# Transposing r, a~ and W of four chunks within partitions, with the transposition finished by DMA over DRAM, in a chunked RWKV-7 plus gated MLP kernel on one Trainium2 core

## The chip, the core and the metric

The kernel runs on one core of one Trainium2 chip. A core has five engines, each with a queue of its own that issues in order: TensorE (PE in the profile; its weight loads are PEld), VectorE (DVE), ScalarE (ACT), GpSimd (POOL) and SyncE (SP). SP computes nothing; nearly all DMAs of this kernel are issued from its queue. The metric is the device time of one execution in microseconds. Three runs of the kernel before took 804.71, 801.88 and 800.59 us, median 801.88.

## The reference, cut to what matters

There are 4 batches and 8 heads, 768 steps and a head dimension of 40. Each head keeps a 40x40 state that every step reads, decays, corrects and extends:

```python
for t in range(S):
    y[:, :, t] = einsum('bhd,bhde->bhe', r[t], state)
    Sa = einsum('bhde,bhe->bhd', state, a[t])
    state = state * w[t][:, :, None, :] - outer(Sa, b[t]) + outer(v[t], k[t])
```

The result, reshaped to 3072 tokens of 320 features, goes through a two-layer block with the activation h cos h:

```python
h = x @ w_in            # 3072x320 by 320x2048
out = (h * cos(h)) @ w_out
```

All is float32.

## The kernel before

**Chunks.** The recurrence is cut into 24 chunks of 32 steps. Within a chunk the steps are worked off as matmuls: W is the running product of w from the chunk's start, a~ is a times W of the step before, b and k are divided by W. So each chunk needs r, a~, W, b/W, k/W and v with the head dimension on the partitions ("transposed": rows 0 to 39 and 64 to 103 hold the even and the odd heads), while DRAM gives them with batch and step on the partitions ("natural", tiles `nat_w`, `nat_a`, `nat_r` and so on, 40 features padded to 64).

**How the transposed form is made.** `turned` (line 327) issues four TensorE transposes of 128x128, two heads each, into a PSUM tile, and ScalarE or VectorE moves the result to SBUF. For W and a~ this goes two chunks at a time in phase 1:
- `p1_w(c)` (362): eight transposes of `nat_w` into `wT`; for chunks from 4 on ScalarE copies each half into a tile `wb` (378); POOL copies the last column of each head into `wc` (380) and writes ones into the first columns (`from_one`, 391). `over_w` (393) takes the reciprocal of the natural W on VectorE and multiplies b by it on POOL.
- `p1_a(c)` (406): eight transposes of `nat_a` into `aps`; VectorE multiplies each half by W into `aT` (`a_W`, 399).
- `p1_b(c)`, `p1_n(c)`: transposes of b/W, then the products of b/W with a~ into `nps`, which ScalarE copies into `nt` (459).

For r and v it is done chunk by chunk in `p2_v(c)` (604): four transposes each, from `vp` and `rp`, which POOL filled from `nat_v` and `nat_r` in `p2_in` (584), and two copies of ScalarE.

**Where W comes from.** For chunks from 4 on the running products are made four chunks at a time. `ws_fetch` (159) loads w of one "quad" into `ws`, a tile with (batch, head, chunk) on the 128 partitions and 32x40 values each; `ws_scan` (166) does nine VectorE multiplications along the steps; `ws_store` (178) writes the products to DRAM (`wd`), from where `load` brings them into `nat_w` chunk by chunk. `scanned(q)` (906) issues the scan, and by `later` the store two steps and the next fetch twelve steps on. It stands in chunk 3 for quad 2, at the end of chunk 4 for quad 3, and near the end of chunks 8 and 12 for quads 4 and 5.

**The order of work.** Nothing is scheduled by a compiler: instructions stand on each queue in the order of the program. For every chunk a list `segs` (lines 1049 to 1101) names the steps: `t` (transposes of the state), `q` (the state read by r), `x`, `s`, `z` (the solve and the new state), `v`, `k`, `g` (the next chunk's inputs and their Gram matrices), the phase-1 steps `pw`, `pa`, `pb`, `pn` of two chunks that lie some chunks ahead, and places `M` for pieces of the two-layer block. The chunks that carry `pw` and `pa` for chunks from 8 on are 4, 5, 7, 9, 11, 13, 15 and 17. `later(n, work)` (343) lets work be issued n steps on; DMAs are placed in this way.

The chain within a chunk that the prediction speaks of: `t` writes the transposed state to PSUM, ScalarE copies it (`s`, 658), `q` multiplies it with r, ScalarE copies that (`qz`, 670), `x` reads it (`x0ps<-qz,aT`), ScalarE and VectorE copy (`x`, 695 and 696), and `s` reads those (`sps`). Each M piece is 8 to 24 matmuls `ph` or `po`; ScalarE and VectorE turn `ph` into `gT` (829 to 839, "turns"). The big PSUM tiles (`wT`, `aps`, `qps`, `nps`, `kT`, `x0ps` and others) share two buffers in turn.

## Time and profile before

| what | value |
| --- | --- |
| runs shown | 800.59, 801.88, 804.71 us |
| profiled execution, from its first to its last instruction | 803.7 us |
| granted TensorE clock, mean | 0.973 |
| TensorE busy | 753.0 us (94%) |
| VectorE, ScalarE, POOL busy | 487.9, 387.2, 200.2 us |
| DMA packets of SP's queue | 177440, 30.1% of 16 engines |
| reciprocal of W on VectorE, 128x320 | 20 of 2.14 us |
| transposes wT, aps, r: median duration | 273 ns |

The profile gives the span of the profiled execution and no separate time of it. Times in a row of the timeline are the start and then the duration; "x8" means that eight equal instructions are shown as one row. Matmuls overlap, so the distance between starts of neighbouring rows says what a group takes from TensorE's queue, and not its duration. A bracket at the end of a row holds the idle time before it on its engine and what ended it. In the windows, each engine's busy time is followed by its number of instructions, and the last three numbers are the granted clock, the DMA share and GB/s. Rows named SPq are SP's DMA issues.

### The profile page before, as it was taken

To read this page: it belongs to the slowest core of one execution; us is meant where nothing else is said; L and a number is where in the kernel's file an instruction comes from. 1 tells how busy PE (TensorE), PEld (TensorE's weight loads), DVE (VectorE), ACT (ScalarE), POOL (GpSimd) and SP (SyncE) were. 2 spreads that over 40 slices of the span, in tenths; PEclk is the share of its full clock that TensorE was granted. 3 is DMA by queue.
4 is the path that set the end of the run, shared out by engine and by line. 5 is a ranking of instruction groups with operands and counts; after the bars stand their busy time and mean duration, and the time that the engine had idled before them with its cause. 6 is when DMAs were issued, how large, how long until landed. Compare 5 with 4: busy or idle time off the path is not lost.

```text
span 803.7 us, 39602 instructions
## 1 busy us (share of the span) xinstructions
PE 753.0 (94%) x17812; PEld 578.6 (72%) x17812; DVE 487.9 (61%) x1025; ACT 387.2 (48%) x723; POOL 200.2 (25%) x354
## 2 busy tenths in 40 slices
PE   4777799999989999999999999999999999999997
PEld 4545577777767777777777787777787777777775
DVE  8879858854634796553895644994346863333231
ACT  1337766554434436545435635534645445354352
POOL 5326634320321220330330230332031122201000
PEclk9778999999999999999999999999999999999999
DMA  8675462443253324334224314223220222001000
GB/s 113 164 187 141 132 171 64 91 93 66 50 122 55 71 40 68 68 99 69 54 44 68 91 40 69 52 44 71 45 46 21 46 46 53 20 16 34 20 17 16
DMA packets 183304, 55.79 MB, mean 69 GB/s; under 512 B 157152, under 2 KB 178656, under 8 KB 183136
## 3 DMA queue, kind: packets, MB, share of 16 engines
q1 hardware_dynamic: 177440, 52.11, 30.1%
q8 instruction: 140, 2.29, 1.2%
q10 hardware_dynamic: 5440, 0.82, 0.7%
q0 software_dynamic: 256, 0.33, 0.3%
q14 instruction: 28, 0.23, 0.1%
HBM read 42.07 MB, written 11.14 MB: 66 GB/s over the span
## 4 chain that ended last, share of the span: by engine, by line
PE 68%; DVE 14%; ACT 5%; DMA 5%; issue 4%; POOL 2%; SPq 2%; DVEq 0%; ACTq 0%; POOLq 0%
PE ph L101 24%; PE po L101 20%; PE x0ps L101 4%; PE dps L101 3%; DVE rw L395 3%; PE gram L101 3%; PE vT L330 3%; PE sps L101 2%; DVE inv_tmp L494 2%; DVE inv L498 2%; PE nps L101 2%; PE qps L101 2%; PE sT L654 1%; SPq L152 1%; PE kT L330 1%
## 5 line engine op out<-in xcount | busy, mean ns | idle before, releaser
L101 PE MATMUL po<-w_out_sb,gT 128*128 128x320 f32 x768 | 223.3, 439 | 0.0
L101 PE MATMUL ph<-xT,w_in_sb 128*128 128x256 f32 x768 | 187.8, 389 | 1.9 <-issue 1.9
L101 PEld LDWEIGHTS po<-w_out_sb,gT 128*128 128x128 f32 x768 | 140.1, 190 | 54.4 <-issue 2.0
L101 PEld LDWEIGHTS ph<-xT,w_in_sb 128*128 128x128 f32 x768 | 140.8, 192 | 31.9 <-issue 14.1
L829 ACT ACTIVATE turns<-ph,rnd 128x512 f32<-128x512 f32 x96 | 64.2, 685 | 159.9 <-PE ph L101 159.5
L831 DVE SCALAR_TENSOR_TENSOR turns<-turns,ph 128x512 f32<-128x512 f32 x96 | 64.1, 683 | 115.3 <-ACT turns L829 115.0
L839 DVE TENSOR_TENSOR gT<-ph,turns 128x512 f32<-128x512 f32 x96 | 65.7, 686 | 39.1 <-ACT turns L836 39.1
L755 POOL TENSOR_TENSOR qz<-qz,wc 128x160 f32<-128x160 f32 x92 | 42.1, 475 | 167.5 <-DVE qz L754 166.8
L836 ACT ACTIVATE turns<-turns,half_pi 128x512 f32<-128x512 f32 x96 | 69.3, 722 | 3.1
L835 ACT ACTIVATE turns<-turns 128x512 f32<-128x512 f32 x96 | 60.2, 627 | 18.9 <-DVE turns L831 18.9
L101 PE MATMUL ph<-xT,w_in_tail 64*128 64x256 f32 (+1 forms) x512 | 55.0, 393 | 2.7 <-issue 2.7
L498 DVE TENSOR_TENSOR inv<-inv,inv_tmp 128x31 f32<-128x31 f32 (+15 forms) x124 | 50.7, 409 | 4.3
L754 DVE TENSOR_TENSOR qz<-dps,qz 128x160 f32<-128x160 f32 x92 | 28.9, 314 | 35.5 <-PE dps L101 35.4
L586 POOL COPY vp<-nat_v 128x320 f32<-128x320 f32 x24 | 12.0, 500 | 153.7 <-DMA nat_v<-in_v_dram 133.1
L494 DVE TENSOR_TENSOR inv_tmp<-u,inv 128x31 f32<-128x31 f32 (+15 forms) x124 | 48.3, 390 | 2.3
L395 DVE RECIPROCAL rw<-nat_w 128x320 f32<-128x320 f32 x20 | 42.8, 2141 | 0.1
L658 ACT COPY s<-sT 128x512 f32<-128x512 f32 x46 | 24.5, 583 | 35.9 <-PE sT L654 35.9
L101 PEld LDWEIGHTS ph<-xT,w_in_tail 64*128 64x128 f32 (+1 forms) x512 | 32.2, 160 | 12.2 <-issue 8.6
L766 POOL TENSOR_TENSOR yt<-yt,wb 128x512 f32<-128x512 f32 x24 | 31.6, 1316 | 22.3 <-DVE yt L761 22.3
L396 POOL TENSOR_TENSOR bn<-nat_b,rw 128x320 f32<-128x320 f32 x22 | 19.9, 906 | 43.9 <-DVE rw L395 37.1
L642 ACT COPY vvm<-gram 128x256 f32<-128x256 f32 x24 | 8.8, 368 | 45.6 <-DVE ag L637 45.2
L718 DVE TENSOR_TENSOR sm<-sps,su 128x128 f32<-128x128 f32 x48 | 11.7, 284 | 31.1 <-ACT sm L713 28.4
(136 smaller groups left out, 1130.6 us busy)
## 6 DMA issues: line engine op xcount, KB each, us to landing
words<-in_moe_w_in_dram SPq DMA_DIRECT2D x8, 512.0 KB
xd<-yt SPq DMA_DIRECT2D x48, 80.0 KB
out_dram<-ot SPq DMA_DIRECT2D x24, 160.0 KB
nat_k<-in_k_dram SPq DMA_DIRECT2D x92, 40.0 KB
nat_v<-in_v_dram SPq DMA_DIRECT2D x92, 40.0 KB
nat_r<-in_r_dram SPq DMA_DIRECT2D x92, 40.0 KB
nat_a<-in_a_dram SPq DMA_DIRECT2D x84, 40.0 KB
ws<-in_w_dram SPq DMA_DIRECT2D x5, 640.0 KB
```

The costliest lines, as they stand in the source:

```text
L101: nc.tensor.matmul(o, lhsT=lhsT, rhs=rhs, start=start, stop=stop, skip_group_check=True)
L330: nc.tensor.transpose(ps[:, i * P : (i + 1) * P], x[:, 2 * i : 2 * i + 2].rearrange("p e d -> p (e d)"), ident)
L395: nc.vector.reciprocal(rw, wn)
L494: nc.vector.tensor_tensor(tmp, u[:, j : j + 1, :j].to_broadcast([P, C - j, j]), x[:, j:, j : j + 1].to_broadcast([P, C - j, j]), ALU.mult,)
L498: nc.vector.tensor_tensor(x[:, j:, :j], x[:, j:, :j], tmp, ALU.subtract)
L755: nc.gpsimd.tensor_tensor(z, z, wc.rearrange("p (f m b) -> p f m b", f=2, m=2)[:, :, :, bb] .unsqueeze(3).to_broadcast([P, 2, 2, D]), ALU. ...
L766: nc.gpsimd.tensor_tensor(yt.rearrange("p j b t -> p (j b) t"), yt.rearrange("p j b t -> p (j b) t"), wx, ALU.mult)
L829: nc.scalar.activation(n, u, ACTF.Identity, bias=rnd, scale=1.0)
L831: nc.vector.scalar_tensor_tensor(n, n, -ROUND, u, ALU.add, ALU.subtract)
L835: nc.scalar.activation(n, n, ACTF.Abs)
L836: nc.scalar.activation(n, n, ACTF.Sin, bias=half_pi, scale=-2.0 * math.pi)
L839: nc.vector.tensor_tensor(gT[:, 2 * e : 2 * e + 2].rearrange("p f t -> p (f t)"), us[e], ns[e], ALU.mult)
```

## The change

From chunk 8 on (`QT = 8`) r, a~ and W aren't transposed by TensorE any more.

- `quad_fetch` loads r or a of four chunks in the layout of `ws` into a tile `raw`. A flip then permutes each partition's 32x40 values to 40x32: `quad_r` and `quad_w` with one ScalarE copy, `quad_a` with one VectorE multiplication, which also makes a~ from a and W, and a small ScalarE copy for the first step. `quad_store` writes the flipped tile to DRAM one step later.
- `fetch_T` reads a chunk of it back, in two DMAs of 40 partitions by 16 runs of 32 values, straight into `wb`, `aT` or `rT`.
- `p1_w` and `p1_a` keep `over_w` for these chunks and issue the fetches instead of the transposes; `own_w` does POOL's share in the b step. `p2_v` transposes v alone. The natural loads of a and r go; those of w, b, k and v stay.
- In `scanned`, `quad_a` follows the scan at once, `quad_w` comes four steps on, and the next fetch goes from 12 to 14 steps. `quad_r` is issued six steps into chunks 5, 9, 13 and 17, its fetch one step into them.
- The free axis of `aT` and `wb` gets another order for these chunks, and the readers follow. The tiles of the weights' rounding (`mant`, `expo`, `sign`) become parts of one tag `cv`, of two buffers, which `raw` and the flips share.

```diff
+    def quad_fetch(n, q, via=nc.sync):
+        raw = sb2.tile([P, C, D], F32, tag="cv", name="raw")
...
+    def quad_tile():
+        return sb2.tile([P, D, C], F32, tag="cv", name="flip")
...
+    def quad_r(n, q):
+        raw, t = G["raw", n], quad_tile()
+        nc.scalar.copy(t, raw.rearrange("p t d -> p d t"))
+        later(1, lambda: quad_store(n, q, t, True))
+
+    def quad_a(q):
+        raw, t = G["raw", "a"], quad_tile()
+        nc.vector.tensor_tensor(
+            t[:, :, 1:], raw[:, 1:].rearrange("p t d -> p d t"),
+            ws[:, : C - 1].rearrange("p t d -> p d t"), ALU.mult,
+        )
+        nc.scalar.copy(t[:, :, 0:1], raw[:, 0:1].rearrange("p t d -> p d t"))
+        later(1, lambda: quad_store("a", q, t, False))
+
+    def quad_w(q):
+        t = quad_tile()
+        nc.scalar.copy(t, ws.rearrange("p t d -> p d t"))
+        later(1, lambda: quad_store("w", q, t, False))
+
+    def fetch_T(n, c, dst, of_heads):
+
+        x = td[n, c // 4][c % 4].rearrange("m (d t) -> d m t", t=C)
+        for e in range(2):
+            at_e = x[:, 4 * B * e : 4 * B * (e + 1)] if of_heads else x[:, e::2]
+            nc.sync.dma_start(dst[half[e]].rearrange("p (m t) -> p m t", t=C), at_e)
...
     def p1_w(c):
+        if c >= QT:
+            if c == 8:
+                later(2, lambda: over_w(c, unpad(nat["w", c])))
+            else:
+                over_w(c, unpad(nat["w", c]))
+            for i in range(2):
+                fetch_aw(c + i, "w")
+            return
...
     def p1_a(c):
+        if c >= QT:
+            over_w(c + 1, unpad(nat["w", c + 1]))
+            for i in range(2):
+                fetch_aw(c + i, "a")
+            return
...
         ws_scan(q)
         later(2, lambda: ws_store(q))
+        n = 12
+        if 4 * q >= QT:
+            quad_a(q)
+            later(4, lambda: quad_w(q))
+            n = 14
         if q + 1 < NCH // 4:
-            later(12, lambda: ws_fetch(q + 1))
+            later(n, lambda: ws_fetch(q + 1))
+            if 4 * q >= QT:
+                later(n, lambda: quad_fetch("a", q + 1))
...
+            if c == 3:
+                later(4, lambda: quad_fetch("a", 2))
+            if c % 4 == 1 and c > 4 and c + 3 < NCH:
+                later(1, lambda c=c: quad_fetch("r", (c + 3) // 4))
+                later(6, lambda c=c: quad_r("r", (c + 3) // 4))
```

## The prediction

> **What bounds the kernel now.** I read the page's busy times and its chain first, then the windows by stage, then the timeline around one `scanned` step, because the change adds its work there.
>
> The page, busy time and the chain by engine:
>
> ```profile
> PE 753.0 (94%) x17812; PEld 578.6 (72%) x17812; DVE 487.9 (61%) x1025; ACT 387.2 (48%) x723; POOL 200.2 (25%) x354
> ...
> PE 68%; DVE 14%; ACT 5%; DMA 5%; issue 4%; POOL 2%; SPq 2%; DVEq 0%; ACTq 0%; POOLq 0%
> ```
>
> Windows by stage, and a gap at 228 us with the windows after it:
>
> ```profile
> 240.00:610.00 370.00, 364.27 (x8886) 283.99 (x8885) 234.73 (x503) 184.04 (x346) 86.55 (x161) 1.00 0.30 60
> ...
> 228.00:231.40 3.40, 0.69 (x5) 0.31 (x4) 1.06 (x6) 0.12 (x1) 3.37 (x6) 1.00 0.45 70
> 231.40:234.80 3.40, 3.40 (x9) 2.52 (x8) 0.69 (x1) 0.57 (x1) 0.50 (x2) 0.50 0.41 67
> ```
>
> From 240 to 610 us, the stage that the change thins out, TensorE is busy 364.27 of 370 us at granted clock 1.00: its issue order sets the end, and each transpose taken out is worth its pitch there. But a gap costs more than itself. After the 2.71 us gap at 228 us the granted clock was 0.50 for 3.4 us, which loses some 1.7 us more.
>
> The timeline where chunk 9 begins, just after `scanned(4)`:
>
> ```profile
> 335.08 1.07 ACT L658 COPY s<-sT 128x512 f32<-128x512 f32 x2 [2.45 <-PE sT L654]
> 335.39 1.81 DVE L175 TENSOR_TENSOR ws<-ws 128x40 f32<-128x40 f32 x4
> ...
> 336.61 1.04 PE L330 MATMUL wT<-ident,nat_w 128*128 128x128 f32 x8
> ...
> 337.57 0.81 PE L101 MATMUL qps<-rT,s 40*40 40x32 f32 x64
> ...
> 338.69 1.19 ACT L670 COPY qz<-qps 40x512 f32<-40x512 f32 x2
> ...
> 341.78 0.40 SPq L180 DMA_DIRECT2D wd<-ws  x1
> ...
> 341.95 0.89 PE L101 MATMUL x0ps<-qz,aT 40*32 40x72 f32 x64
> ...
> 346.21 0.59 SPq L161 DMA_DIRECT2D ws<-in_w_dram  x1
> ```
>
> The scan on VectorE ends at 337.20. ScalarE is free from 336.15, and its `qz` copies end at 339.88; TensorE reads `qz` at 341.95, 2.07 us later. That slack is all there is. The last row, the next fetch into `ws`, waited for the store at 341.78: 640 KB take 4.4 us from issue until a waiter goes on. SP's own waits say the same of two such stores (in total, times, longest), and in chunk 5 SP is the busy one:
>
> ```profile
> SPq L161 <- DMA wd<-ws: 5.1, 2, 3.9
> ```
>
> ```profile
> 215.06 2.90 SPq L152 DMA_DIRECT2D nat_k<-in_k_dram  x4
> ...
> 218.22 0.88 PE L101 MATMUL x0ps<-vvm,ag 32*32 32x72 f32 x64
> ```
>
> **What the change takes away.** The transposes, start to start: eight of wT 336.61 to 337.57 = 0.96 us; eight of aps 352.85 to 353.73 = 0.88; four of r 346.81 to 347.24 = 0.43. The duration rows (273 ns each) overlap and would give over twice that. Gone are 8 pairs of wT and aps and 16 r sets: 8 x 0.96 + 8 x 0.88 + 16 x 0.43 = 21.6 us, all on the bounding engine. Off the path go 16 `wb` copies (0.59) and 16 `rT` copies (0.60) of ScalarE, 16 aT products of VectorE (0.67) and 16 `rp` copies of POOL (0.5): that relief I count at nothing, as its engines idle 39% and more; the small waits behind such copies (the gaps before vT are 0.4 to 0.6 us) bound it at 4 us gained.
>
> **What it adds, and what hides it.** SP: 64 loads of a and 64 of r go, 96 transposed fetches, 24 stores and 8 quad fetches come: 128 against 128, at about 0.49 us an issue no change in sum. Packets: 32768 of 160 B go, 61440 of 128 B come. The queue's 30.1% of 16 engines over 177440 packets is 21.8 ns a packet, so 28672 more are 39 us of one engine's share over some 400 us: DMA share 0.30 becomes about 0.40. Fetches lie a chunk (29 us) ahead of their readers, so hidden; if that cover goes, `nps` waits for aT by the lateness. POOL's own-partition work (`wc`, ones) moves from the W step to the b step, with `yt` as its reader ten us on: nothing. The renamed tiles of the rounding (`cv` for mant, expo, sign) keep their two buffers: nothing.
>
> **What is not hidden: waits on ScalarE's queue.** `cv` has two buffers, and the built program gives these waits. `flip` of W (ScalarE, 128x1280) waits until the store of the a~ `flip` has landed, for quads 3, 4 and 5; `flip` of r waits until the W store has landed. ScalarE issues in order; behind the W flip stand the two `qz` copies (quads 4, 5) or the turns and `nt` copies (quad 3), and TensorE waits for these.
>
> No row shows the flips. The VectorE flip, 1240 elements: 128x640 took 815 ns, so 1.6 us; the strided transposition (1947 ns for 1024) makes it 2.4. The ScalarE flip, 1280 elements: 583 ns for 512 makes 1.5; the `nt` copy, which writes with a stride, 625 ns for 256, makes 3.1. Both flips write in order and read with a stride, so I take 1.6 and 1.5, nearest to rows with ordered writes. The Trainium skill, SBUF — State Buffer, "Door 1: The DMA port swizzle", has 16-byte lines and a penalty for each access that crosses to a new one; every read here is 160 B from the last. By it the flips would sit at the upper ends, and the sum would be about 8 us longer; no row here has such a read alone.
>
> Quad 4 (chunk 9): scan 337.20 + 1.6 = 338.8; SP's v loads run until 339.70, so the store goes out at 339.75; + 4.4 = 344.2 landed; + 1.5 flip = 345.7; + 1.2 `qz` = 346.9. Due: 341.95 - 0.96 (no wT) = 341.0. TensorE stalls 5.9 us. Bounds: landing 3.5 and issue at 338.8 give 4.0; landing 5.5 and flip 3.1 give 8.5.
> Quad 5 (chunk 13): the same with scan end 453.57 and SP free at 453.99: 455.2, 459.6, 461.1, 462.3; due 458.31 - 0.96 = 457.4: 4.9 (4.0 to 8.3).
> Quad 3 (chunk 5): here SP is the late one. In the trace the W and k loads end at 217.96; the a~ store is queued behind them, about 217.4 with the wT step gone. + 4.4 = 221.8; flip 223.3; two turns 1.4, Abs and Sin 1.35, two `nt` copies 1.05: 227.1. x0ps needs the PSUM buffer that `nt` frees; due 218.22 - 1.84 = 216.4. I take 10.3 of the 10.7, as some lateness of the loads shrinks (7.3 to 14). Then the W store stands behind raw r, 4 v, `wd`, 4 r and 8 b issues, 18 x 0.49, and each waits for the DMA eight before it, 10 us: 227.5, landed 231.9, r flip to 233.4, then Abs, Sin, kT and x copies 2.3 and VectorE's x 0.45: 236. TensorE reaches sps at 227.1 + 1.63 + 2.35 = 231: 4.4 to 5; I take 4.4 (1 to 8).
> Quad 2 (chunk 3): no landing to wait for; VectorE's flip stands ahead of gT and sm, and aps waited for sm there already (0.41): 1.6 (0 to 3). Quad 5 of r, chunk 17: waits only for old work: 0 (to 1.5).
> Clock: four gaps of over 2 us, each up to 1.7 us at half clock: 5 (1.7 to 6.8). The gap at 228 us with its half clock cost 4.4 us and falls into chunk 5's new stall; the profile names no releaser, so I give half of it back, -2.2 (-4.4 to 0). The Trainium skill, TensorE: Matmul & The Clock Gate, "What's actually happening", puts the drop after an idle window of about 3.4 us; here 2.71 us was enough, so the row is used. By the page only chunk 5's gap and the longer of the others would count, and the clock term would be some 3 us.
>
> Sum: 5.9 + 4.9 + 10.3 + 4.4 + 1.6 + 5 - 2.2 = 29.9 against 21.6: +8.3 us. The profiled execution has a span of 803.7 us, inside the runs shown (800.59 to 804.71) and 1.8 above their median, 801.88. So 810.2 in terms of the median. All low ends: 4.0 + 4.0 + 7.3 + 1 + 0 + 1.7 - 4.4 = 13.6, -8.0, 794; all high ends: 8.5 + 8.3 + 14 + 8 + 3 + 6.8 + 1.5 = 50.1, +28.5, 830.
>
> **Rivals.**
> 1. Faster: chunk 5's two waits do not reach TensorE, since SP comes to the a~ store sooner than the trace of before lets me think (it loses eight a loads right there, 218.07 to 227.85). Then 17.2 us of losses (10.3 + 4.4 + 2.5 of clock) and the -2.2 are out: 5.9 + 4.9 + 1.6 + 2.5 = 14.9 against 21.6, 795. It is faster by over 0.5% (797.9) as long as chunk 5 costs under 2.7 us. Against it: the store has 12 W and k issues in front either way.
> 2. Faster still: ScalarE never holds TensorE, say because stores land in under 1 us; 1.6 of loss: 782. Against it: the 4.4 us row, and a waits row of SP with 3.9 us for the same store.
> 3. Slower still: 640 KB bursts (store, `wd`, raw r, raw a within 10 us) delay each landing. DMA share was 0.72 at 220 GB/s in 224.5 to 228. Two us more at six waits: 822, and 826 or more with the high flips.
> 4. Near break-even: chunk 5 and the clock at their low ends, 7.3 + 1 + 1.7 = 10.0 in place of 10.3 + 4.4 + 5 = 19.7: 810.2 - 9.7 = 800.5.
> That the transposes stay is no rival: the built program no longer issues them.
>
> **How the numbers follow.** Forecast 0.50 (806 to 822), rival 3 0.12, rival 4 0.16, rival 1 0.14, rival 2 0.08. About 0.5%, 4 us, is what a measurement can tell: slower 0.62, same 0.16, faster 0.22. Predicted 810.2. The range 790 to 827 leaves out rival 2 and the top of rival 3, about 0.1 to 0.15; the forecast's own range is 806 to 822.
>
> **What would show it.** Right: no wT or aps rows after 200 us; a `flip<-ws` row on ScalarE whose idle before it, 5 us and more, ends with DMA td; x0ps waiting for `qz` once each in chunks 9 and 13, and once for `nt` in chunk 5; PEclk 0.5 behind these; 240 to 610 us shorter only in chunks without a flip. Wrong: flips that start at once, or stalls under 2 us: then the 21.6 us come through, and the queue reading was at fault. Flips over 2.5 us would make it worse than 820.

## The result and the profile after

The changed kernel takes 845.6 us (842.3 to 847.9) against 802.7 (800.6 to 804.7) of the kernel before: a ratio of 1.0525, interval 1.0491 to 1.056. It is slower, as forecast, but by 43 us and not by 8, and it lies outside the range. The profiled execution has a span of 840.4 us, 36.7 more than that of before.

From the page, busy times and the chain by engine:

```profile
PE 746.9 (89%) x17620; PEld 564.7 (67%) x17620; DVE 479.8 (57%) x1013; ACT 393.1 (47%) x703; POOL 191.1 (23%) x338
...
PE 53%; DVE 18%; ACT 9%; DMA 7%; issue 6%; SPq 4%; POOL 2%; ACTq 0%; DVEq 0%; POOLq 0%
```

TensorE's part of the chain fell from 68% to 53%. The 15 points went to the engines and the DMAs that TensorE now waits for. The next two fences are windows from the transposes that open chunk 5 to those that open chunk 19 (columns as in the prediction: length, busy time of PE, PEld, DVE, ACT and POOL, then clock, DMA share, GB/s), of the kernel before and of the changed one:

```profile
206.50:625.60 419.10, 410.33 (x10068) 319.51 (x10068) 261.92 (x565) 203.87 (x382) 98.17 (x179) 1.00 0.31 62
```

```profile
206.20:659.70 453.50, 404.67 (x9909) 309.20 (x9909) 260.54 (x554) 209.83 (x365) 92.77 (x172) 0.95 0.39 86
354.20:357.70 3.50, 0.03 (x2) 0.00 (x0) 0.75 (x1) 1.30 (x1) 0.86 (x1) 0.99 1.04 354
357.70:364.50 6.80, 4.73 (x73) 3.47 (x74) 2.34 (x4) 5.34 (x8) 0.00 (x0) 0.50 0.95 247
364.50:371.30 6.80, 3.16 (x76) 2.23 (x75) 1.18 (x3) 5.23 (x7) 0.00 (x0) 1.00 0.29 77
371.30:374.70 3.40, 3.40 (x24) 1.76 (x30) 0.00 (x0) 0.14 (x1) 0.00 (x0) 0.50 0.75 244
```

Length less busy time is TensorE's idle time: 8.8 us before, 48.8 after. The other four rows are chunk 9. Two stalls bring half clock, 6.8 and 3.4 us long: the first stretch begins at 357.7, inside a stall that lasts until 359.61 (timeline below), the second at 371.3, 1.1 us behind the end of another. I split the stage of 14 chunks into three: idle time; loss by the clock, which is half of the time at clock 0.50 during which a matmul ran; and the rest, work at full clock.

| chunks 5 to 18, us | length | idle | clock | work |
|---|---|---|---|---|
| before | 419.1 | 8.8 | 1.7 | 408.6 |
| after | 453.4 | 48.8 | 12.8 | 391.8 |
| change | +34.3 | +40.0 | +11.1 | -16.8 |

The missing transposes are there, 16.8 us of them in this stage. TensorE gave them back more than twice over by waiting. In the timeline of chunk 9 (start, duration; the bracket is the idle time before the row and what ended it) one sees how:

```profile
350.32 2.57 DVE L212 TENSOR_TENSOR flip<-raw,ws 128x1240 f32<-128x1240 f32 x1
...
352.95 0.58 SPq L200 DMA_DIRECT2D td<-flip  x1
...
356.40 2.67 ACT L221 COPY flip<-ws 128x1280 f32<-128x1280 f32 x1 [7.17 <-DMA td<-flip]
358.98 1.18 ACT L763 COPY qz<-qps 40x512 f32<-40x512 f32 x2
...
359.61 0.45 PE L101 MATMUL x0ps<-qz,aT 40*32 40x72 f32 x2 [5.38 <-ACT qz L763]
...
361.04 0.86 SPq L200 DMA_DIRECT2D td<-flip  x1
...
365.68 2.67 ACT L207 COPY flip<-raw 128x1280 f32<-128x1280 f32 x1 [2.38 <-DMA td<-flip]
...
369.54 0.56 ACT L710 COPY kT<-kT 128x512 f32<-128x512 f32 x1
...
370.16 0.66 PE L383 MATMUL vT<-ident,vp 128*128 128x128 f32 x4 [3.64 <-ACT kT L710]
```

ScalarE stands 7.17 us until the a~ store has landed (352.95 to 356.40, 3.45 us), flips W for 2.67, and only then copies `qz`. The W store (361.04 to 365.68, 4.6 us) then holds the r flip, and this one holds kT. The chain of landing, flip, store and landing runs twice through ScalarE's order in one chunk. The page's waits say how often (in total, times, longest):

```profile
ACT flip L221 <- DMA td<-flip: 25.9, 3, 10.9
...
PE x0ps L101 <- ACT qz L763: 12.0, 5, 6.0
PE x0ps L101 <- ACT nt L546: 11.9, 1, 11.9
PE vT L383 <- ACT kT L710: 10.1, 6, 3.9
...
ACT flip L207 <- DMA td<-flip: 9.5, 3, 4.9
```

Six gaps of TensorE of over 3 us make 34.5 of the 40.0 us: 11.9 and 3.6 in chunk 5, 5.4 and 3.6 in chunk 9, 6.05 and 3.9 in chunk 13.

### The profile page after: what moved, and what is told of

Its sections match the earlier page's. It is cut to its first block, busy times and chain, and to the rows that moved or that the text cites. A ratio compares the mean times of both kernels' runs of the same rounds, so it can differ in the third digit from the quotient of the medians.

```text
span 840.4 us, 39041 instructions
## 1 busy us (share of the span) xinstructions
PE 746.9 (89%) x17620; PEld 564.7 (67%) x17620; DVE 479.8 (57%) x1013; ACT 393.1 (47%) x703; POOL 191.1 (23%) x338
## 4 chain that ended last, share of the span: by engine, by line
PE 53%; DVE 18%; ACT 9%; DMA 7%; issue 6%; SPq 4%; POOL 2%; ACTq 0%; DVEq 0%; POOLq 0%
PE ph L101 20%; PE po L101 16%; PE dps L101 3%; PE x0ps L101 3%; DVE inv_tmp L581 3%; DMA td<-flip 2%; PE gram L101 2%; DVE inv L585 2%; DVE rw L456 2%; SPq L155 2%; PE sps L101 2%; ACT turns L928 1%; PE qps L101 1%; DVE turns L923 1%; PE nps L101 1%
## 5 line engine op out<-in xcount | busy, mean ns | idle before, releaser
L101 PE MATMUL po<-w_out_sb,gT 128*128 128x320 f32 x768 | 230.6, 450 | 0.0
L101 PEld LDWEIGHTS po<-w_out_sb,gT 128*128 128x128 f32 x768 | 144.4, 196 | 57.5 <-issue 7.1
L101 PEld LDWEIGHTS ph<-xT,w_in_sb 128*128 128x128 f32 x768 | 142.6, 194 | 31.1 <-issue 12.1
L848 POOL TENSOR_TENSOR qz<-qz,wc 128x160 f32<-128x160 f32 x92 | 41.9, 470 | 259.4 <-DVE qz L847 258.7
L847 DVE TENSOR_TENSOR qz<-dps,qz 128x160 f32<-128x160 f32 x92 | 28.9, 314 | 40.0 <-PE dps L101 39.7
L673 POOL COPY vp<-nat_v 128x320 f32<-128x320 f32 x24 | 11.9, 496 | 137.3 <-DMA nat_v<-in_v_dram 89.9
L457 POOL TENSOR_TENSOR bn<-nat_b,rw 128x320 f32<-128x320 f32 x22 | 19.9, 907 | 96.8 <-DVE rw L456 88.2
L101 PE MATMUL x0ps<-qz,aT 40*32 40x72 f32 x1472 | 23.1, 243 | 14.9 <-ACT qz L763 11.7
L101 PE MATMUL x0ps<-vvm,ag 32*32 32x72 f32 x1536 | 21.8, 232 | 13.0 <-ACT nt L546 11.9
```

Source lines behind the costliest of these rows:

```text
L101: nc.tensor.matmul(o, lhsT=lhsT, rhs=rhs, start=start, stop=stop, skip_group_check=True)
L847: nc.vector.tensor_tensor(z, pick(dp, 0, (2 * N72 + C, 2), (N72, 2), (1, D)), z, ALU.add)
L848: nc.gpsimd.tensor_tensor(z, z, wc[:, :, :, bb].unsqueeze(3).to_broadcast([P, 2, 2, D]), ALU.mult,)
```

## The experiments

All runs in one table: the time, the lengths of the six chunks that matter (from one chunk's first transposes of `sT` to the next's), and the ledger of chunks 5 to 18 as above. The profile of each run is one execution; a few tenths of a chunk are within what differs between executions, and a break inside a group of matmuls (last section) can move a chunk by 1 to 3 us.

| run | us | 5 | 6 | 9 | 10 | 13 | 14 | idle | clock | work |
|---|---|---|---|---|---|---|---|---|---|---|
| before | 802.7 | 38.5 | 30.0 | 28.2 | 29.1 | 28.2 | 28.9 | 8.8 | 1.7 | 408.6 |
| after | 845.6 | 51.0 | 31.0 | 40.7 | 28.4 | 39.9 | 28.5 | 48.8 | 12.8 | 391.8 |
| e1 flips in order | 833.6 | 49.1 | 31.2 | 37.6 | 28.4 | 39.1 | 28.5 | 38.6 | 15.5 | 391.6 |
| e2 no flips | 807.6 | 32.0 | 38.6 | 30.3 | 28.4 | 30.0 | 28.5 | 21.4 | 7.1 | 392.4 |
| e3 r alone | 820.8 | 40.9 | 29.9 | 29.5 | 28.5 | 33.5 | 29.5 | 20.9 | 5.0 | 404.8 |
| e4 a~, W alone | 809.1 | 36.9 | 30.9 | 30.4 | 30.0 | 29.6 | 28.9 | 17.0 | 3.4 | 397.5 |
| e5 third buffer | 838.9 | 50.9 | 30.6 | 37.1 | 28.5 | 36.0 | 28.5 | 41.9 | 12.8 | 391.2 |
| e6 flips on POOL | 828.6 | 33.7 | 41.4 | 27.1 | 40.0 | 27.3 | 36.8 | 38.4 | 6.3 | 393.3 |
| e7 stalls filled | 842.2 | 57.6 | 30.4 | 37.6 | 29.0 | 39.1 | 29.4 | 22.8 | 11.5 | 420.5 |
| e8 a~, W, all on POOL | 805.2 | 32.0 | 38.2 | 27.5 | 32.3 | 26.5 | 28.9 | 15.9 | 4.4 | 396.8 |
| e9 e8, POOL stores, later | 797.8 | 31.5 | 35.9 | 26.5 | 31.7 | 27.1 | 29.1 | 13.4 | 3.2 | 394.4 |
| e10 e6, POOL stores | 823.5 | 32.8 | 37.8 | 30.4 | 37.5 | 28.3 | 37.1 | 33.1 | 9.5 | 393.4 |
| e11 e8, later | 803.6 | 30.9 | 38.1 | 26.9 | 35.7 | 26.5 | 29.2 | 14.8 | 6.4 | 394.3 |
| e12 r alone, POOL | 813.3 | 40.6 | 29.9 | 27.9 | 28.9 | 28.7 | 29.5 | 13.8 | 2.9 | 405.8 |
| e13 issued later | 818.3 | 38.3 | 34.9 | 28.8 | 36.1 | 27.7 | 30.1 | 27.1 | 6.7 | 394.8 |
| e14 later, on POOL | 825.9 | 32.9 | 42.9 | 27.0 | 32.7 | 27.4 | 34.5 | 29.5 | 10.4 | 391.9 |
| e15 a~, W, later | 802.2 | 33.8 | 32.7 | 27.4 | 31.1 | 28.8 | 29.0 | 15.9 | 0.0 | 396.0 |

**e1: what do the strided reads cost?**

```diff
-        nc.scalar.copy(t, raw.rearrange("p t d -> p d t"))
+        nc.scalar.copy(flat(t), flat(raw))
```

and the same for the flips of a~ and W.

> The three flips copy in order instead of transposing (same sizes, same stores, same waits; the output is therefore not the reference's). Theory S, strided reads: in the changed kernel the flips took 2.57 us on VectorE and 2.67 on ScalarE; rows of the kernel before with ordered operands make that about 1.6 and 1.5. In chunks 9 and 13 the first stall is then shorter by 1.0 + 1.2 = 2.2 us and the second (the r flip) by 1.2; in chunk 5 1.2 + 1.2; in chunk 3 1.0. Sum 10.2 us off 845.6, 835, and down to 830 if a half-clock stretch shortens with its gap. Rival L, landings alone: the store's issue and landing set the end and a flip's length is hidden in them: 842 to 846.

The flips' rows (engine, operation, then duration in ns as least, median, most), of the changed kernel and then of e1:

```profile
L212 DVE TENSOR_TENSOR flip<-raw,ws x4: 2565/2568/2582, 148.5 to 476.8; 128x1240 f32<-128x1240 f32 x4
L221 ACT COPY flip<-ws x4: 2672/2672/2691, 151.1 to 483.6; 128x1280 f32<-128x1280 f32 x4
L207 ACT COPY flip<-raw x4: 2672/2672/2684, 234.8 to 610.2; 128x1280 f32<-128x1280 f32 x4
```

```profile
L212 DVE TENSOR_TENSOR flip<-raw,ws x4: 1449/1449/1451, 148.8 to 471.4; 128x1240 f32<-128x1240 f32 x4
...
L218 ACT COPY flip<-ws x4: 1258/1258/1260, 150.4 to 476.5; 128x1280 f32<-128x1280 f32 x4
L207 ACT COPY flip<-raw x4: 1257/1257/1262, 233.5 to 603.7; 128x1280 f32<-128x1280 f32 x4
```

A read that jumps 160 B per element costs VectorE 1.12 us and ScalarE 1.41 us more for the same elements. The kernel took 833.6 us (ratio to before 1.040, 1.035 to 1.045), 12 less than the changed one. The flip's length is not hidden in the landings: theory S holds in the sum, and the other 31 us have another cause. By chunk it is rougher: chunk 9 became 3.1 us shorter, but chunk 13 only 0.8, since its second stall grew from 3.94 to 5.21 us and the half clock behind it from 3.4 to 6.8.

**e2: no flip at all.** The raw blocks and the running product are stored as they are, so a~ also lacks its product with W:

```diff
-        raw, t = G["raw", n], quad_tile()
-        nc.scalar.copy(t, raw.rearrange("p t d -> p d t"))
+        t = G["raw", n].rearrange("p t d -> p d t")
```

> No flip at all: raw a~ (without its product with W), raw r and the running product are stored as they are, so the output is not the reference's; the stores, fetches and the removal of the transposes stay. Theory W, waits on ScalarE: chunks 5, 9 and 13 lengthened by 12.5 + 12.5 + 11.7 = 36.7 us because the flips wait there for landings; with no flip that goes, and the 2.2 us or so of transposes missing in each of them show: 845.6 - 36.7 - 3 x 2.2 - 2.5 (the r flip of chunk 17) - 1.1 (chunk 3) = 799, and 785 at the lowest if the flips also disturbed the chunks between. Rival T, traffic: the 640 KB stores and fetches and the 128-byte packets delay other landings by themselves: most of the growth of chunks 5, 9 and 13 stays, 820 or more. The removal alone, as forecast, would make 781.

807.6 us, 1.008 of before (1.0046 to 1.0115). The 38 us that went are the flips and what waits on their account, as theory W has it; but 807.6 is 27 over the 781 that the removal alone promised, and TensorE's work is 16.2 us less than before. Part of rival T is therefore true too. The windows of e2 show where:

```profile
228.00:232.00 4.00, 4.00 (x21) 3.07 (x20) 3.03 (x4) 2.83 (x5) 0.23 (x1) 1.00 0.73 278
232.00:235.00 3.00, 2.79 (x139) 2.07 (x137) 1.29 (x3) 0.54 (x2) 0.87 (x1) 1.00 0.87 271
235.00:238.00 3.00, 0.00 (x0) 0.00 (x0) 2.19 (x2) 0.91 (x2) 0.73 (x1) 1.00 0.79 279
```

The 640 KB of ws and of raw a~ are issued at 231.10 and 231.74, and the store of `xd`, which `ph` needs as `xT`, at 232.43. `xT` could be fetched only from 239.53 to 241.10, and `ph` stood still in chunk 6 for 6.99 us until 241.78. Of the 6.8 us at half clock from 239.2 on, 4.3 lie behind it. The profile puts this gap to no releaser; that it is xT is read from SP's rows (in e6 below a like gap is named). With the stalls of chunk 5 gone, TensorE meets a burst there that it did not meet before. Of the 12.6 us of new idle time in chunks 5 to 18 this gap makes 7.0; 5.1 are breaks inside groups of matmuls (7.85 us against 2.71 before), which the last section explains.

**e3 and e4: one part alone.** In e3 a~ and W go through TensorE as before, in e4 r does.

```diff
+    QA = 99
...
     def p1_w(c):
-        if c >= QT:
+        if c >= QA:
```

and so in every place that is about a~ and W.

> Only r goes over DRAM; a~ and W are transposed on TensorE as before. Theory W: the r flip waits for no earlier store here, only for raw r; it costs its 2.67 us on ScalarE in chunks 5, 9, 13 and 17, of which 1 to 2.7 us reach TensorE each, against 16 x 0.43 = 6.9 us of transposes gone: 797 to 803. Rival T, traffic: eight more fetches of 128-byte packets a quad and the burst of raw r delay other landings, or the gain is lost as it was in the chunks without flips of the changed kernel: 803 to 810.

```diff
+    QR = 99
...
-        if c < QT:
+        if c < QR:
             turned(ps[:, 1], rp)
```

and so in every place that is about r.

> Only a~ and W go over DRAM; r is transposed on TensorE as before. Theory W: the stalls before x0ps (5.4 and 6.05 us in chunks 9 and 13, 11.9 in chunk 5) with their half clock stay; the second ones (3.6 us before vT in chunks 9 and 13, 3.6 before sps in chunk 5, 2.5 in chunk 17, and 1.7 us of half clock behind three of them) go, 845.6 - 13.3 - 5 = 827, and 6.9 us of r transposes come back: 834. Rival C, coupling: without r's traffic the a~ and W stores land earlier and the first stalls shrink too by 1 to 2 us each with their clock: 824 to 829.

e3 took 820.8 us (1.024, 1.016 to 1.032) and e4 809.1 (1.011, 1.006 to 1.016). Both expectations missed. r alone costs 18.5 us (two runs; 13 to 26 by the interval), more than a~ and W alone with 6.8, though it removes 3.8 us of work; and 18.5 + 6.8 = 25 is 18 short of the 43 of both together. The stalls of a~ and W need r for most of their length. In e4 no raw r and no r flip share the two `cv` buffers, so that the W flip waits for no landing, and the stalls before x0ps in chunks 9 and 13 are 1.4 and 1.95 us in place of 5.4 and 6.05. Rival C named such a coupling, but by r's traffic, and its lower end was still 15 us above the result; e5 tells buffers from traffic.

**e5: take away what makes the W flip wait.** For quads 4 and 5 it writes into memory that is free by then:

```diff
+    spare = const.tile([P, 2 * H * DP + H * D], F32, tag="spare", name="spare")
...
     def quad_w(q):
-        t = quad_tile()
+        if q < 4:
+            t = quad_tile()
+        else:
+            t = spare[:, : D * C].rearrange("p (d t) -> p d t", t=C)
```

> As the changed kernel, but the W flips of quads 4 and 5 write into memory that is free by then (the a~ and r tiles of the first eight chunks), not into the buffer whose store must land first. Theory B, the buffer: ScalarE's W flip then waits for the scan alone; the stalls of 5.4 and 6.05 us before x0ps in chunks 9 and 13 go with some 2.4 + 2.0 us of half clock, and the r flip behind costs 1.6 to 2.9 us as in the run with r alone, in place of 3.6 and 3.9: 845.6 - 15.9 - 2.5 = 827. Rival T, traffic: raw r lands no sooner, TensorE comes to the second wait some 5 us earlier and waits there for what it was spared: 838 to 842.

The timeline of e5, chunk 9:

```profile
356.99 0.88 PE L101 MATMUL x0ps<-qz,aT 40*32 40x72 f32 x64
...
364.86 2.67 ACT L213 COPY flip<-raw 128x1280 f32<-128x1280 f32 x1 [4.87 <-DMA raw<-in_r_dram]
...
369.34 1.11 PE L392 MATMUL vT<-ident,vp 128*128 128x128 f32 x4 [7.91 <-ACT kT L719]
```

The stall before x0ps is gone, with not a tenth left. The one before vT has grown from 3.64 to 7.91 us, now for raw r, issued at 356.92. In chunks 9 and 13 the stalls before x0ps lost 11.4 us, so the buffer made them, and those before vT grew by 7.4. The time is 838.9 us: most of what the first wait gave, the second took. Rival T's 838 to 842 is the better of the two.

**e6, e10: the flips on another engine, then their stores on another queue.**

```diff
-        nc.scalar.copy(t, ws.rearrange("p t d -> p d t"))
+        nc.gpsimd.tensor_copy(t, ws.rearrange("p t d -> p d t"))
```

> As the changed kernel, but POOL does the W and r flips, in the same places; the a~ flip stays on VectorE and all stores, waits and buffers stay. In the changed kernel POOL idles from 342.4 to 355.0 and from 355.9 to 376.6 us in chunk 9. Theory Q, the in-order queue of ScalarE: qz, nt, turns, kT and x no longer stand behind a wait for a landing, so the stalls of chunks 5, 9, 13 and 17 (11.9 + 3.6 + 5.4 + 3.6 + 6.05 + 3.9 + 2.5 = 37 us) and their half clock (13 us) go: 796, or 808 if the wait of 7 us for xT in chunk 6 that the run with no flips had shows here too. Rival P: POOL is held in ScalarE's place, and qz, yt, bn or vp are late: 820 or more.

POOL flips in 2.67 us, no slower than ScalarE. Chunks 5, 9 and 13 become shorter than in the kernel before, so the wait did sit in ScalarE's order. But the time is 828.6 us: chunks 6, 10 and 14 are 8 to 11 us longer. The timeline of e6 at the end of chunk 9:

```profile
361.83 2.67 POOL L207 COPY flip<-raw 128x1280 f32<-128x1280 f32 x1 [8.04 <-DMA td<-flip]
...
364.46 1.69 POOL L848 TENSOR_TENSOR qz<-qz,wc 128x160 f32<-128x160 f32 x4
364.53 2.83 SPq L203 DMA_DIRECT2D td<-flip  x4
...
366.10 1.28 POOL L858 TENSOR_TENSOR yt<-yt,wb 128x512 f32<-128x512 f32 x1
...
374.12 0.90 SPq L867 DMA_DIRECT2D xd<-yt  x2
...
377.06 0.39 SPq L877 DMA_DIRECT2D xT<-xd  x1
...
379.32 2.90 PE L101 MATMUL ph<-xT,w_in_sb 128*128 128x256 f32 x6 [9.61 <-DMA xT<-xd]
```

The wait for the W store moved to POOL, in front of qz and yt; yt is done at 367.4, but SP gets to `xd` only at 374.1, behind the r store, two fetches of 640 KB and four of aT. Two orders hold the step, and e10 takes one away:

```diff
-            nc.sync.dma_start(to.rearrange("c m x -> m c x"), x)
+            nc.gpsimd.dma_start(to.rearrange("c m x -> m c x"), x)
```

> As the run with the W and r flips on POOL (828.6), and POOL's queue, not SP's, issues the eight kinds of store of the flipped quads. In that run chunks 5, 9 and 13 were 4.8, 1.1 and 0.9 us shorter than in the kernel before, and chunks 6, 10 and 14 10 to 11, 11 and 8 us longer, with ph waiting 10.1, 9.6 and 5.2 us for xT; SP's store of the r flip waited there for POOL, and xd and xT stood behind it. Theory SP: SP's order is what turned the flips' lateness into ph's wait; with the stores elsewhere chunks 6, 10 and 14 come back to 31, 29 and 29: 828.6 - 11.4 - 10.9 - 7.9 = 798. Rival P: POOL itself holds the r flip back for the W store (8.0 us in chunk 9), and qz, yt and so xd are late with it: 815 or more. Rival T: bursts ahead of xd delay it: chunk 6 alone keeps its 10 us, 808.

823.5 us. Chunk 6 gained 3.6 of the 11.4 us, chunk 10 2.5, chunk 14 nothing. SP's stores were not the main holder. POOL's own wait remains (28.6 us for six landings), which is rival P, and SP's fetch of raw a~ still waits 9.3 us for POOL's flip.

**e7: the clock.** Idle matmuls in the six stalls, planned at 0.095 us each (they took 0.084 to 0.088, so the fills ended early):

```diff
-        FILL = {..., (3, 4): 20}
+        FILL = {..., (3, 4): 20, (5, 8): 119, (5, 10): 33, (9, 5): 53, (9, 9): 34, (13, 5): 59, (13, 9): 37}
```

> As the changed kernel, with idle matmuls of 0.095 us each issued where TensorE stalls: 119 and 33 in chunk 5, 53 and 34 in chunk 9, 59 and 37 in chunk 13, a little shorter than the stalls. Theory K: the half clock behind the stalls is set by TensorE's idleness alone: with the six stalls filled it stays at 1.0, and 2.4 + 2.7 + 2.45 + 1.7 + 2.0 + 1.7 = 13 us go: 833. Rival N: the idle matmuls do not hold the clock, or they delay what they were to cover: 845 or more.

Windows of e7 in chunk 9:

```profile
360.50:366.90 6.40, 6.37 (x123) 5.81 (x121) 2.73 (x2) 2.22 (x1) 0.86 (x1) 1.00 0.70 234
367.90:371.30 3.40, 3.10 (x74) 2.43 (x75) 1.28 (x2) 3.17 (x6) 0.00 (x0) 1.00 0.90 163
371.30:374.70 3.40, 3.38 (x89) 2.69 (x89) 1.05 (x2) 1.38 (x2) 0.00 (x0) 1.00 0.81 204
378.10:381.50 3.40, 3.40 (x75) 2.49 (x79) 0.67 (x3) 0.91 (x3) 0.00 (x0) 1.00 0.58 178
```

The clock stays at 1.00 through a chunk that had 10.2 us at 0.50, and the chunk is 3.1 us shorter (40.7 to 37.6): idleness sets the clock, as theory K says. Yet the whole gained 3.4 and not 13 us, and with two runs of 840.5 and 843.9 against 842.3 to 847.9 even that is hardly clear of the spread. In chunk 5 gaps of 3.1 and 1.0 us were left and a break of 1.4 us came (last section), with 17 us at half clock; chunk 13 kept a gap of 2.0 with 3.4 us of half clock. A TensorE that is not slowed may also arrive sooner at the next wait for a landing; that is argued and was not measured.

**e13, e14: issue the same steps later.** e6 and e10 had left open whether order or landings hold the step. e13 is the changed kernel with three numbers edited:

```diff
-            later(4, lambda: quad_w(q))
-            n = 14
+            later(10, lambda: quad_w(q))
+            n = 20
...
-                later(6, lambda c=c: quad_r("r", (c + 3) // 4))
+                later(14, lambda c=c: quad_r("r", (c + 3) // 4))
```

> As the changed kernel, with three steps issued later and nothing else: the W flip 10 steps after the scan in place of 4, the r flip 14 steps into its chunk in place of 6, the next fetches into ws and raw a~ 20 steps after the scan in place of 14. Theory O, order: ScalarE meets each flip after the landing that it waits for, so it is held by 2.7 us of copying alone; of the 37 us of stalls in chunks 5, 9, 13 and 17 some 8 to 11 stay, and of the 13 us of half clock 3 to 5, and SP's stores no longer wait for late flips: 845.6 - 27 - 9 = 810. Rival T, bursts and landings: ph then waits for xT in chunks 6, 10 and 14 as it did with the flips on POOL: 825 or more.

818.3 us (1.019, 1.014 to 1.024): 27 of the 43 us are gone by order alone, and chunks 5, 9 and 13 are back at the lengths of before. The rest sits in chunks 6 and 10, 4.9 and 7 us longer. In chunk 9 the r flip still waits for the W store, but that now holds up nothing that TensorE needs at once. In chunk 5 it does: ScalarE stands 10.78 us for the same landing, `rt` and `rT` come late, and `gram` has gaps of 2.35 and 2.10 us just before chunk 6, with 10.2 us at half clock from 245.1 on. The timeline of e13, chunks 5 and 9:

```profile
238.73 2.67 ACT L207 COPY flip<-raw 128x1280 f32<-128x1280 f32 x1 [10.78 <-DMA td<-flip]
...
246.42 0.89 PE L101 MATMUL gram<-rT,vT 40*32 40x32 f32 x64 [2.10 <-ACT rT L704]
...
353.06 2.69 ACT L221 COPY flip<-ws 128x1280 f32<-128x1280 f32 x1
...
363.31 2.68 ACT L207 COPY flip<-raw 128x1280 f32<-128x1280 f32 x1 [7.07 <-DMA td<-flip]
364.46 0.99 SPq L867 DMA_DIRECT2D xd<-yt  x2
```

Theory O's 810 was too hopeful by 8, rival T's 825 too dark by 7. What is left is only in small part rival T's: the half clock in chunk 6, 4.0 of its 4.9 us, comes of order in chunk 5; chunk 10 has a break of 3.06 us (last section) with 6.8 us at half clock; and `ph` waits for xT for 3.8 us in all.

> The same later issue, the W and r flips on POOL as well, and no tiny matmuls ahead of chunk 19. With the flips on POOL at their old places it was 828.6, chunks 6, 10 and 14 being 11.4, 10.9 and 7.9 us longer than in the kernel before. Theory O: POOL and SP meet the flips and stores late enough not to wait: these 30 us go, 797 to 800. Rival T: xT's store still lands behind 640 KB bursts: 812 or more.

e14, which also leaves out 60 tiny idle matmuls ahead of chunk 19, took 825.9 us, hardly less than e6. `ph` waits for xT in five places there, 16.7 us in all, where e13 has three and 3.8. The same steps at the same places do worse on POOL, which also makes qz and yt, on which xd depends. Theory O fails for POOL.

**e8, e9, e11, e15: a~ and W alone, made as good as possible.** e8 is e4 with all its flips on POOL. e9 also lets POOL issue the stores, issues the next fetches into ws and raw a~ 18 steps after the scan, and drops the 60 tiny matmuls ahead of chunk 19; e11 is e9 with SP's stores; e15 keeps VectorE and ScalarE and issues the W flip later. Of e8:

```diff
     def quad_a(q):
-        nc.vector.tensor_tensor(
+        nc.gpsimd.tensor_tensor(
```

> Only a~ and W over DRAM, r by TensorE, and all three flips on POOL. The run with only a~ and W (flips on VectorE and ScalarE) took 809.1; its profile has left: 2.8 us before aps in chunk 3, 4.2 before x0ps in chunk 5, 1.4 and 1.95 before x0ps in chunks 9 and 13, and three stretches of 3.4 us at half clock behind these. Theory Q: these are the flips' place on two busy queues; on POOL they go, 809.1 - 10.3 - 5.1 = 794, under the kernel before. Rival T: they are landings and bursts, or POOL is slower at strided reads and holds bn, qz and yt: 804 to 815.

Of e9 and e11, e9 with the stores as in e10:

```diff
-            n = 14
+            n = 18
...
-        N_PAD = {0: 0, 19: 60}
+        N_PAD = {0: 0, 19: 0}
```

> As the run with a~ and W alone and all flips on POOL (805.2); POOL issues their stores; the next fetches into ws and raw a~ are issued 18 steps after the scan in place of 14; and the 60 tiny matmuls ahead of chunk 19 are left out. Theory: that run's chunks 6 and 10 were 8.2 and 3.2 us longer than in the kernel before, ph waiting 6.1 and 1.7 us for xT, whose store landed behind 640 KB each of ws, raw a~ and W; chunk 19 was 4.1 us longer by a gap of 2.2 us inside sps that nothing in the profile explains and a half clock behind it, which should move with the number of instructions ahead. All gone: 805.2 - 8.2 - 3 - 4 = 790. Rival: TensorE, with less to do, waits elsewhere for the same landings: 798 to 803.

> The same as the run before in this call, but SP issues the stores as in the changed kernel. Theory burst: xT's wait in chunk 6 came from the 1.9 MB issued just ahead of xd, so the later fetches alone remove it: 790 to 793, no more than 2 us from the other. Rival SP: SP held by a store that waits for POOL's flips (5.3 and 2.7 us) delays xd whatever lies ahead: 798 to 802.

Of e15, beside the two edits above:

```diff
-            later(4, lambda: quad_w(q))
+            later(10, lambda: quad_w(q))
```

> Only a~ and W over DRAM, flips on VectorE and ScalarE as in the changed kernel, the W flip 10 steps after the scan, the next fetches 18, no tiny matmuls ahead of chunk 19. The run without these three edits took 809.1, with 4.2, 1.4 and 1.95 us before x0ps in chunks 5, 9 and 13, each with 1.7 us of half clock or near it, and 4 us more in chunk 19. Theory O: all of that goes, 809.1 - 7.5 - 4 - 4 = 794, as good as the best run so far (797.8) without POOL. Rival: the a~ flip on VectorE (2.6 us, in front of sm and gT) and the flip's 2.7 us on ScalarE remain: 800 to 805.

e8 took 805.2 us (1.005, 1.0021 to 1.0079): the stalls of chunks 3, 5, 9 and 13 went, and a gap of 6.06 us before `ph` came in chunk 6, which ends 0.6 us after SP has issued the last fetch of xT. e11 took 803.6 (1.0007, 0.9971 to 1.0044): with the fetches later `ph`'s gap is 1.5 us, but `nps` waits 3.3 us there for the landing of aT. The two fetches of 640 KB now stand in front of aT's (241.40 and 242.09, aT from 242.74), so the burst has moved from one reader to another. In chunk 10 e11 has a break of 2.39 us (last section). e9 took 797.8 us, 0.9923 of before (0.9892 to 0.9954), the one run that beats it; 15 us were expected of its edits, and 7.4 came. e15 took 802.2 (1.0003, 0.9977 to 1.003): no gap over 1.5 us is left in chunks 5 to 18 and no half clock, but the VectorE flip's gap in chunk 3 stays (2.28 us and a half clock behind it). A window of e9 over chunks 5 to 18:

```profile
204.40:615.40 411.00, 397.57 (x9896) 306.74 (x9897) 252.23 (x549) 197.69 (x368) 124.91 (x199) 0.99 0.39 82
```

That is 8 us shorter than before with 14.2 us less work: 4.6 us of new idle time and 1.5 us of clock are still there.

**e12: r alone, its flip on POOL.**

```diff
-        nc.scalar.copy(t, raw.rearrange("p t d -> p d t"))
+        nc.gpsimd.tensor_copy(t, raw.rearrange("p t d -> p d t"))
```

> Only r over DRAM, its flip on POOL in place of ScalarE. With the flip on ScalarE it took 820.8, 18.5 over the kernel before, though 6.9 us of transposes went. Theory Q: the flip, 2.7 us behind a wait of up to 2.5 us for raw r, holds ScalarE's kT and x: in chunks 5, 9, 13 and 17 that run was 2.4, 1.3, 5.3 and 1.7 us longer; on POOL these 10.7 go: 810. Rival T: raw r's bursts and r's fetches delay other landings, xT's above all, and take the place: 817 or more.

813.3 us (1.011, 1.008 to 1.014). Chunks 9, 13 and 17 lost 1.6, 4.8 and 1.6 us, chunk 5 almost nothing, 8 in all. Of the 8.3 us by which its span (812.0) exceeds that of before, 3.5 lie in chunks 5 to 18 and 4.7 behind them. Breaks inside groups of matmuls, such as one of 1.95 us inside sps in chunk 19, make 9.3 us from chunk 5 on, against 2.7 before; the last section comes to them.

## Why the prediction was right and wrong

**What failed.** The forecast was +8.3 us, the profiled execution is 36.7 longer. Of the 28.4 us between them the r flips, priced at nothing outside chunk 5, are 8.9; the clock 9.5; small waits and breaks, counted at nothing, 9.5; the stalls that were priced 2.3; and the removal 1.7, less 2.2 for the gap at 228 us, which went wholly. That is 29.7, 1.3 too much, which is about what the gaps under 1 us became shorter by.

**Right in kind.** Slower, with a~'s landing as the wait in front of the W flip, `qz` and `nt` behind it, and half clock behind the gaps. The first stalls were nearly right: x0ps before qz 5.9 against 5.38 us measured, 4.9 against 6.05; before nt 10.3 against 11.9; sps 4.4 against 3.6; aps in chunk 3 1.6 against 2.9 less the 0.4 of before. The six stores on which flips waited landed in 3.45 to 4.64 us; 4.4 was taken. That 5.9 came so near to 5.38 is partly luck: the two flips took 2.1 us more than was taken, but the landing 1.0 less, the store's issue 0.9 less, and TensorE needed only the first of the two `qz` copies, 0.6 less.

**Right in size: the removal.** By the same starts, seven pairs at 1.84 us and twelve r sets at 0.43 in chunks 5 to 18 are 18.0 us; TensorE's work fell by 16.8. From chunk 3 on it fell by 19.9, so most of the 21.6 us were there.

**Wrong: the r flips of chunks 9 and 13.** The prediction wrote down that the r flip waits for the landed W store, and priced it in chunk 5 alone. In chunks 9 and 13 it held kT and so vT for 3.64 and 3.94 us, 7.6 in all. In chunk 17, taken at nothing with a bound of 1.5, it cost 1.34. It was the second half of one chain, and e4, which has no r, shows what hung on it: 845.6 - 809.1 = 36.5 us, since r's buffers make the first wait too (e5).

**Wrong: the flips' duration.** Taken 1.6 and 1.5 us, from rows with ordered writes; measured 2.57 and 2.67, above and below the upper bounds named (2.4 and 3.1). It is the read's stride that costs, as e1 shows with 12.0 us. The Trainium skill, SBUF — State Buffer, "Door 1: The DMA port swizzle", states a penalty for each access that crosses to a new 16-byte line. The measurement agrees in direction: reads 160 B apart took 2.57 and 2.67 us, ordered ones 1.45 and 1.26. The 8 us that the prediction worked out from it were a third too low.

**Wrong: the clock.** Priced as four gaps of up to 1.7 us, 5 in all. There were six, and a gap can bring more than one stretch: 13.7 us at half clock in chunk 5, of which 8.9 lie inside the stall and cost nothing, and 6.8 in chunks 9 and 13. The loss was 1.7 to 2.7 us a gap. It grew by 11.1 us in chunks 5 to 18, though the 1.7 behind the gap at 228 us went, and chunk 20 has a stretch of 3.4 us more.

**Wrong: the relief, counted at nothing with a gain as its bound.** In chunks 7, 11 and 15 sps waits 1.2 us for VectorE's `x`, where it waited up to 0.5 before. In chunk 7 that `x` waits for ScalarE's, and this one stands behind `turns` that VectorE reaches late, behind the reciprocal of W and steps of the inverse. These had been there before; that the wT transposes between had given them 0.96 us is argued from the order. In chunk 6 bT waits 1.2 us for POOL's `bn`. Gaps of 1.06, 1.15 and 1.16 us in chunks 8, 9 and 17 and of 1.33 in chunk 20 are breaks of the kind that the last section tells of.

**What of the sum.** In chunks 5 to 18: six stalls 34.5, the r flip of chunk 17 1.3, the waits for `x` and `bn` 4.8, breaks 3.4, less the gap at 228 us, which went altogether (2.7 us; the prediction gave back half of it and its half clock, and the last section says what it was), and less 1.3 in gaps under 1 us, makes 40.0 us of idle time. Clock 11.1, work -16.8.

**The rivals.** 1, 2 and 4 fell, since ScalarE held TensorE in every quad. Of rival 3 the mechanism is there (three blocks of 640 KB at DMA share 1.04 in the window at 354.2), but the stores that it wanted 2 us later landed in 3.45 to 4.64 us. It shows elsewhere: at xT in e2 and e6, and at raw r in e5, 7.9 us after its issue.

What stays open is whether an r path could pay at all with its own third buffer and with POOL free of qz and yt, which was not tried. That r alone on POOL (e12) is still 10 us over before is mostly breaks: in the profiled executions breaks are 6.6 and the loss by clock 4.3 us more than before, of 12.1 to be explained (8.3 us longer with 3.8 us less work).

## What to carry to other kernels

When work moves from a bounding engine to a chain of DMA, permutation and DMA, price every link of the chain in every place where it occurs, and look for the instruction that waits in order ahead of something urgent: issuing the same steps six to eight steps later brought back 27 of 43 us here, more than another engine (17), another buffer (7) or contiguous reads (12). A removed instruction also removes cover: the next waits of TensorE stand right behind it. And two chains that share buffers and an engine's order can cost more together than apart, as parts of 18.5 and 6.8 us made 43.

## What the runs showed of the hardware that was not expected

**Half clock after short gaps.** A gap of 1.33 us at 693.8 us of the changed kernel was followed by 3.4 us at 0.50; in e7 gaps of 1.02 and 2.17 us in chunk 9 were not, and one of 2.00 in chunk 13 was. Every stretch is 3.4 us or a multiple, up to the one that the program's end cuts off. In each of the 17 traces the clock changes only on a grid of 3.413 us that stays fixed for the execution. Over chunks 3 to 22 of all traces, the clock fell after 72 windows of this grid: after every one in which a matmul ran for less than 43.5% of the window (47, nine of them without any), after 25 of 118 between 43.5 and 73.5%, and after none of 2739 above. So it counts how a gap lies on the grid: the gap of 2.00 us lies in one window (499.97 to 503.39, busy 41%), that of 2.17 is cut by a border at 377.09 (65 and 71%). The Trainium skill, TensorE: Matmul & The Clock Gate, "What's actually happening", speaks of a free-running window of about 3.4 us that must be idle; the fixed grid agrees with that, but a wholly idle window was not needed here.

**Breaks inside a group of matmuls.** e9 and e11 issue the same matmuls, and both break in chunk 20's `gram` after 55 of 62 matmuls. The timelines of e9 and of e11:

```profile
650.00 0.66 PE L101 MATMUL gram<-rT,vT 40*32 40x32 f32 x55
652.28 0.26 PE L101 MATMUL gram<-rT,vT 40*32 40x32 f32 x7 [1.62 <-issue]
```

```profile
655.83 0.66 PE L101 MATMUL gram<-rT,vT 40*32 40x32 f32 x55
656.65 0.26 PE L101 MATMUL gram<-rT,vT 40*32 40x32 f32 x7 [0.15 <-issue]
```

The same instruction waits 1.62 us in the one and 0.15 in the other, and half clock follows only the long wait; chunk 20 is 3.2 us longer for it. The page of the changed kernel has this row of the instruction queue (packets, MB, share of 16 engines):

```profile
q8 instruction: 138, 2.26, 1.1%
```

That is 16 KB a packet, and a packet for every 256 of the 35475 matmuls and weight loads, counted together. In the 17 traces 227 gaps of TensorE of 0.25 us or more, from 60 us on, end with no releaser. Five are the wait for xT in chunk 6. The other 222 all stand at the same place of a block of 256 such instructions, and each ends 1.2 to 2.0 us (median 1.4) after a packet of this queue has landed: in e9 the packet moved from 649.89 to 650.85 and the break ended at 652.28, in e11 from 653.89 to 655.26 and at 656.65. So TensorE waits there for its code, and the break is long where the packet is late. The Trainium skill, Runtime: NRT & Kernel Launch, "Instruction fetch mechanics", has code come in blocks of 16 KiB, 256 instructions, mostly hidden; the spacing agrees, and breaks of up to 3.1 us (e13, chunk 10) are not hidden. The gap of the kernel before at 228 us is such a break too: it ends 1.5 us after a packet that landed at 229.26.

An edit that adds or removes matmuls moves the blocks. From chunk 5 on breaks make 2.7 us in the kernel before, 5.8 in the changed one and 2.5 to 10.6 in the other runs, with half clock behind some, so a difference of a few us between two kernels can be theirs. No run moved the blocks alone.

**POOL's strided copy is as fast as ScalarE's**, 2.67 us for 128x1280 (e6), but its product with a stride takes 5.26 us (e8) against VectorE's 2.57.
